# FFN layer 1 with fixed PSUM banks and a first output summed in PSUM, four layernorms on another engine, and shifted due times of the attention

## The chip, the core and the metric

The kernel runs on one core of a Trainium2 chip. The metric is the time of one execution in device microseconds (us), median of three runs. The core has five engines with a queue each, worked off strictly in the written order: TensorE (PE, with its weight loads, PEld), VectorE (DVE), ScalarE (ACT), GpSimd (POOL) and SyncE (SP), which issues nearly all DMAs. An instruction waits on semaphores that other engines or DMAs raise; everything behind it on its own engine waits with it.

## What is computed

The input x has 2048 tokens of 576 features. A parallel block is added to it:

```python
xn = layernorm(x)
out = x + A(xn) + B(xn)
# A: qkv = xn @ wqkv, 32 heads of 18; each token attends to itself and to
#    7 earlier tokens at distances 2, 4 .. 14; softmax; o @ wo
# B: h = xn @ w1 + b1 (4608 hidden); act = h * tanh(softplus(h)); act @ w2
```

Everything is float32. A product of two float32 matrices is made of three matmuls of rounded parts (high x high, low x high, high x low).

## The kernel before, in words

The tokens are worked in two halves (`hf` 0 and 1) of 1024, each of two blocks `b` of 512 tokens, each block of four tiles `jj` of 128. All matrix products run on PE; a schedule `plan`, a list of slots written out by hand, says in which order. A slot holds its PE work (`fns`) and background work (`before(i, fn)`: weight casts, attention steps, DMAs). The last loop of `block_kernel` walks the slots and emits, per slot, `first` (the exponentials that an attention step left for the next slot), then `bg`, then `held` (the activations that the slot before left in `pend`), then `fns`. For one slot, part 0 of quad (0, 1), `fns` comes ahead of `held`. At the end each engine is bound to this program order.

The stages, in order: a head (`prologue`, `first_item`) that normalises the first four tiles one by one (`ln_stats`, `ln_root`, `ln_newton`, `ln_norm`; lines 151 to 184), transposes them on PE (`ln_transpose`, `transpose_split`) and multiplies them by the first QKV weights; the rest of QKV; 18 quads of FFN; the second half's QKV, in part as `z_part`; 18 quads again; and the output projection (`wo_part`).

**A quad** (`hf, q`) is one 2x2 block product of FFN layer 1, computed with seven products of sub-blocks in place of eight. `m1_part` (line 715) issues it in six parts over three PSUM banks of 512 columns: `cur[1]`, `cur[2]`, `cur[3]`. Part 0 sums A11*B11 (6 matmuls, `prod`) in bank 1, ACT copies it to SBUF (`take`, line 691, "c11"), and A12*B21 with a rest (8 matmuls, `prod` and `rest`) goes into bank 2; then `mish` has DVE add c11 to bank 2 (line 702), ACT apply Mish with the bias (line 703), ACT round it to a high part (line 708) and POOL form the low part (line 709). Part 1 starts bank 3 (6 matmuls). Parts 2 and 3 go on in bank 1, with a copy each ("c21", "c22"); parts 4 and 5 finish banks 3 and 1. DVE's sums with c22 and c21 both read bank 3. Between the parts stand slots of FFN layer 2 of the quad before (`m2_pair`, line 755, or `p_item`, line 847, or `m2_cols`, line 868), whose sums DVE adds up (lines 759, 853, 871).

All these PSUM banks come from one tag "h" with four buffers, given out in turn as they come free; QKV, transposes, `z_part` and the projection use the same four. A second tag "out" has the other four.

**Attention** is a generator of 72 steps a half (POOL multiplies, lines 534 and 572; DVE reduces, lines 539 and 578; ACT exponential, line 559). The planner gives every slot a weight (`PART`, `US`), scales it by a `rate` for each stretch between `marks`, sums the weights up to `total`, and puts step n of 146 at the first allowed slot (`ok`) where the sum passes n/146 of the total, one step to a slot.

Of the kernel before, what the change touches and what calls it, by code (L numbers as in the profile page):

```python
# [39 lines left out]
def block_kernel(ctx: ExitStack, tc: tile.TileContext, x, wq, wo, w1, b1, w2, mask, out):  # L40
# [24 lines left out]
    warm = ps.tile([P, 512], F32, tag="h", bufs=4, name="warm")  # L65
# [3 lines left out]
    def transpose_split(src, dst, col, extra=None, pair=False):  # L69
        n = next(tpn)  # L70
        if pair:
            ta, tb = (ps.tile([P, 512], F32, tag="out", bufs=4, name=f"tt{k}_{n}") for k in range(2))
        else:
            ta = ps.tile([P, 512], F32, tag="h", bufs=4, name=f"ta_{n}")
            tb = ps.tile([P, 512], F32, tag="h", bufs=4, name=f"tb_{n}")
        for k in range(KT):
            nc.tensor.transpose(ta[:, k * P:(k + 1) * P], src[:, k * P:(k + 1) * P], ident)
# [5 lines left out]
        nc.scalar.copy(hi, tav)  # L83
        nc.vector.tensor_sub(dst[:, 5:5 + KT, col:col + P], tav, hi.bitcast(F32))
# [4 lines left out]
        nc.vector.tensor_sub(hr[64:P], tbv[64:P], hr[64:P].bitcast(F32))  # L89
# [74 lines left out]
    def ln_newton(n0):  # L164
        g = group[n0]
        k, rs, ve, y, nm = g["k"], *(g[w][:, 0:g["k"]] for w in ("rs", "ve", "y", "nm"))
        if k == 1:
            r, v, y, m = rs[:, 0], ve[:, 0], y[:, 0], nm[:, 0]
            nc.vector.tensor_scalar(y, r, r, v, op0=ALU.mult, op1=ALU.mult)
            nc.vector.tensor_scalar(y, y, -0.5, 1.5, op0=ALU.mult, op1=ALU.add)  # L170
            nc.vector.tensor_scalar(r, r, y, None, op0=ALU.mult)
            nc.vector.tensor_scalar(m, g["mv"][:, 0, 0:1], r, -1.0, op0=ALU.mult, op1=ALU.mult)
        else:
            newton(rs, ve, y)
            nc.vector.tensor_mul(nm, g["mv"][:, 0:k, 0:1], rs)
            nc.vector.tensor_scalar(nm, nm, -1.0, None, op0=ALU.mult)

    def ln_norm(n):
# [3 lines left out]
        nc.scalar.activation(xn[:, 0:D], accs[0][n], AF.Identity, bias=g["nm"][:, i, :], scale=g["rs"][:, i, :])  # L182
# [145 lines left out]
    def qkv_item(hf, g, b, jj, mid=None, mid_at=4):  # L328
# [7 lines left out]
        if (g, b, jj) == (NQ - 1, 0, JB - 1):  # L336
            pq = ps.tile([P, 512], F32, tag="out", bufs=4, name=f"pq_{n}_{jj}")
        else:
            pq = ps.tile([P, 512], F32, tag="h", bufs=4, name=f"pq_{n}_{jj}")
# [85 lines left out]
    def z_part(hf, jj, part):  # L425
        X0, X1 = XTs[hf, 0], XTs[hf, 1]
        tok = slice(jj * P, (jj + 1) * P)
        if part == 0:
# [5 lines left out]
            if jj == JB - 1:  # L434
                zq["h"] = [ps.tile([P, 512], F32, tag="out", bufs=4, name=f"z{n}_{jj}")[:, 0:432] for n in (1, 3)]
                zq["h"].append(ps.tile([P, 512], F32, tag="h", bufs=4, name=f"z2_{jj}")[:, 0:432])
            else:
                zq["h"] = [ps.tile([P, 512], F32, tag="h", bufs=4, name=f"z{n}_{jj}")[:, 0:432] for n in (1, 3, 2)]
# [211 lines left out]
    def bank(hf, q, n):  # L650
        cur[n] = ps.tile([P, TB], F32, tag="h", bufs=4, name=f"h{n}_{hf}_{q}")
        return cur[n]

    def prod(ph, wt, off, X, hi, lo, first, last):
        seq = [(off + k, wl, xs + k) for k in range(2) for wl, xs in ((0, hi), (0, lo), (1, hi))]
        for i, (wk, wl, xs) in enumerate(seq):
            nc.tensor.matmul(ph, wt[:, wl, wk * P:(wk + 1) * P], X[:, xs, :],  # L657
# [8 lines left out]
    seven = lambda hf, q: hf == 1 and q <= 2 * OC  # L666
    rawact, rslot, held_, owner, where = {}, {}, {}, {}, {}
# [47 lines left out]
    def m1_part(hf, q, part):  # L715
# [168 lines left out]
    def o_split(p, step, early=False):  # L884
        hf, j = divmod(2 * p, TJ)
        if step == 0:
# [4 lines left out]
            if early:  # L891
                od["t"] = [ps.tile([P, 512], F32, tag="h", bufs=4, name=f"ot{k}_{p}") for k in range(3)]
# [145 lines left out]
    def wo_part(p, part):  # L1038
# [8 lines left out]
        if part == 0:  # L1047
            od["h"] = [ps.tile([P, 512], F32, tag="h", bufs=4, name=f"o{n}_{p}")[:, 0:HC] for n in (1, 3, 2)]
# [127 lines left out]
    def prologue():  # L1176
# [19 lines left out]
    def first_item(n):  # L1196
# [3 lines left out]
        def mid():  # L1200
# [276 lines left out]
    for q in range(2 * OC + 2):  # L1477
        for i in range(spot(1, q, 0), spot(1, q, 9) + 1):
# [3 lines left out]
             spot(1, 2, 0), spot(1, 2 * OC + 2, 0), spot(1, NP - 1, 0), at["o", 0, 0], at["o", 2, 0]]  # L1482
    rate = (1.15, 0.4, 0.5, 0.8, 1.15, 1.3, 1.2, 0.8, 1.5, 0.8, 0)
# [4 lines left out]
    total = T[at["o", 2, 0]]  # L1488
# [95 lines left out]
```

## Time and profile before

| | us |
|---|---|
| median of 3 runs (lowest, highest) | 1124.1 (1123.77, 1124.33) |
| span of the profiled execution, first to last instruction | 1121.6 |
| median less span | 2.5 |
| PE busy / PEld busy | 1109.5 / 1023.0 |
| DVE busy / POOL busy / ACT busy | 829.0 / 787.7 / 492.1 |

How to read the lines that follow. The page groups instructions: line of the kernel, engine, operation, out<-in by the program's names, shape, count, then busy time and mean of one in ns, then the idle time of the engine just before. A row of the timeline has the start in us from the span's beginning, the duration, engine, line, operation and count; a bracket at its end tells how long the engine idled before and what ended that. A row of the waits says which engine and line waited for which other, us in total, how often, and the longest. Matmuls are pipelined: the duration of one includes its way through the array, while the next begins earlier.

### The profile page before, as it was taken

How to read it: one execution, taken by the hardware profiler on the slowest of the kernel's cores; microseconds unless marked ns; L12 is line 12 of the kernel's file. 1: busy time of each engine (PE TensorE's matmuls, PEld its weight loads, DVE VectorE, ACT ScalarE, POOL GpSimd, SP SyncE). 2: the span in 40 equal slices, each digit the busy share in tenths (PEclk: the TensorE clock that was granted, in tenths of full speed). 3: DMA queues.
4: the chain of work that ended last, by engine and by line, in shares of the span. 5: the costliest groups of instructions: out<-in, count | busy, mean ns of one | idle time of the engine just before them, and what ended most of it. 6: DMA issues, size and time to landing. Idle time of an engine off the chain costs nothing.

```text
span 1121.6 us, 18415 instructions
## 1 busy us (share of the span) xinstructions
PE 1109.5 (99%) x6630; PEld 1023.0 (91%) x6630; DVE 829.0 (74%) x1351; ACT 492.1 (44%) x892; POOL 787.7 (70%) x639
## 2 busy tenths in 40 slices
PE   8999999999999999999999999999999999999998
PEld 7999899999999999899999889999999999999998
DVE  6368788888888888877655456687866677776876
ACT  5544645544554545455233355343433343443332
POOL 2488767767689687676788476665789878668632
PEclk9999999999999999999999999999999999999999
DMA  6899885868767849666596797655655477676463
GB/s 200 283 312 318 290 283 205 289 228 284 261 240 258 282 163 345 222 240 214 191 342 238 231 373 249 241 200 174 227 198 189 168 263 269 215 253 248 157 222 104
DMA packets 147487, 271.08 MB, mean 242 GB/s; under 512 B 30114, under 2 KB 86724, under 8 KB 147396
## 3 DMA queue, kind: packets, MB, share of 16 engines
q1 hardware_dynamic: 147396, 269.91, 69.2%
q8 instruction: 52, 0.85, 0.3%
q14 instruction: 39, 0.32, 0.1%
HBM read 160.39 MB, written 109.48 MB: 241 GB/s over the span
## 4 chain that ended last, share of the span: by engine, by line
PE 89%; DVE 4%; POOL 3%; DMA 2%; issue 1%; ACT 1%; DVEq 0%; POOLq 0%; SPq 0%
PE h L657 28%; PE po L755 19%; PE pq L349 11%; PE po L868 10%; PE po L847 7%; PE h L663 5%; PE o L1056 4%; PE z L447 2%; DMA acc<-in_x 1%; POOL accP L856 1%; DVE u L801 1%; POOL pr L534 0%; DVE accP L871 0%; POOL act L709 0%; DMA z_B<-kept_wq 0%
## 5 line engine op out<-in xcount | busy, mean ns | idle before, releaser
L755 PEld LDWEIGHTS po<-w,act 128*128 128x128 f32 x1728 | 236.4, 188 | 7.5 <-DVE acc L759 1.7
L755 PE MATMUL po<-w,act 128*128 128x288 f32 x1728 | 240.8, 295 | 1.4 <-DVE acc L759 1.2
L534 POOL TENSOR_TENSOR pr<-q,kv 128x576 f32<-128x576 f32 x128 | 195.7, 1553 | 18.7 <-DMA q<-q_d 16.9
L572 POOL TENSOR_TENSOR pv<-L,kv 128x576 f32<-128x576 f32 x128 | 174.3, 1461 | 38.7 <-DVE L L565 20.9
L709 POOL TENSOR_TENSOR act<-c,act 128x512 fp32r<-128x512 f32 x81 | 107.1, 1322 | 128.4 <-ACT act L708 125.5
L759 DVE TENSOR_TENSOR acc<-po,acc 128x288 f32<-128x288 f32 x288 | 120.4, 450 | 31.6 <-PE po L755 30.2
L349 PE MATMUL pq<-wq,xt 128*128 128x432 f32 x672 | 136.2, 361 | 1.8 <-ACT xt L83 1.8
L868 PEld LDWEIGHTS po<-w,act 128*128 128x128 f32 x960 | 131.1, 188 | 3.7 <-DVE accP L871 0.4
L868 PE MATMUL po<-w,act 128*128 128x288 f32 x960 | 133.8, 295 | 0.2
L349 PEld LDWEIGHTS pq<-wq,xt 128*128 128x128 f32 x672 | 125.0, 188 | 8.7 <-ACT xt L83 2.7
L703 ACT ACTIVATE c<-c,b1c 128x512 f32<-128x512 f32 x81 | 58.7, 724 | 132.9 <-DVE c L702 132.6
L657 PE MATMUL h<-xt,t 128*128 128x512 f32 x432 | 110.6, 391 | 0.9 <-DVE c L702 0.8
L657 PE MATMUL h<-S,t 128*128 128x512 f32 x432 | 110.4, 391 | 0.0
L691 ACT COPY c<-h 128x512 f32<-128x512 f32 x81 | 47.4, 586 | 136.5 <-PE h L663 78.3
L578 DVE TENSOR_REDUCE og<-pv 128x144 f32<-128x1152 f32 x64 | 85.9, 1343 | 25.4 <-POOL pv L572 25.4
L657 PE MATMUL h<-xt,wa 128*128 128x512 f32 x432 | 104.0, 390 | 0.0
L657 PEld LDWEIGHTS h<-xt,wa 128*128 128x128 f32 x432 | 80.9, 188 | 16.9
L871 DVE TENSOR_TENSOR accP<-po,accP 128x288 f32<-128x288 f32 x160 | 69.6, 454 | 36.1 <-PE po L868 34.5
L847 PEld LDWEIGHTS po<-pw,u 128*128 128x128 f32 x672 | 92.4, 188 | 2.9 <-DVE u L801 0.5
L847 PE MATMUL po<-pw,u 128*128 128x288 f32 x672 | 94.2, 296 | 0.3 <-DVE u L801 0.3
L539 DVE TENSOR_REDUCE L<-pr 128x64 f32<-128x1152 f32 x64 | 85.8, 1341 | 11.2 <-POOL pr L534 11.1
L657 PEld LDWEIGHTS h<-xt,t 128*128 128x128 f32 x432 | 79.0, 188 | 16.1 <-DVE c L702 1.1
(231 smaller groups left out, 1840.5 us busy)
## 6 DMA issues: line engine op xcount, KB each, us to landing
kv<-kv_d SPq DMA_DIRECT2D x64, 396.0 KB, 5.2
kept_t<-t SPq DMA_DIRECT2D x36, 512.0 KB, 5.3
t<-kept_t SPq DMA_DIRECT2D x36, 512.0 KB, 5.4
rw<-in_w SPq DMA_DIRECT2D x36, 320.0 KB, 4.6
kept_wa<-wa SPq DMA_DIRECT2D x18, 640.0 KB, 3.5
kept_w<-w SPq DMA_DIRECT2D x20, 576.0 KB, 4.8
wa<-kept_wa SPq DMA_DIRECT2D x18, 640.0 KB, 6.1
w<-kept_w SPq DMA_DIRECT2D x20, 576.0 KB, 4.5
```

What stands on the lines that cost most here:

```text
L349: nc.tensor.matmul(pq[:, 0:432], XT[:, xi, tok], wt[wi][:, hl, 0:432], start=i == 0, stop=i == len(seq) - 1)
L534: nc.gpsimd.tensor_tensor(out=pr[:, x:x + hh], in0=q[:, j0 + x:j0 + x + hh, None, :].to_broadcast([P, hh, W, CU]), in1=win(kt, 0, CU, j0 + ...
L539: nc.vector.tensor_reduce(L[:, k, j0:j0 + hj].rearrange("p j w h -> p (j w h)"), pr.rearrange("p j w (h d) -> p (j w h) d", h=2), axis=AX, ...
L572: nc.gpsimd.tensor_tensor(out=pr[:, x:x + hj].rearrange("p j d w -> p j w d"), in0=L[:, k, x:x + hj, :, h:h + 1].to_broadcast([P, hj, W, DH]),
L578: nc.vector.tensor_reduce(og[:, :, c0:c0 + DH], pr, axis=AX, op=ALU.add)
L657: nc.tensor.matmul(ph, wt[:, wl, wk * P:(wk + 1) * P], X[:, xs, :], start=first and i == 0, stop=last and i == len(seq) - 1, skip_group_ch ...
L709: nc.gpsimd.tensor_tensor(out=a[:, 1, :], in0=t, in1=a[:, 0, :].bitcast(F32), op=ALU.subtract)
L755: nc.tensor.matmul(po, acts[hf, q, b, j][:, al, tok], done["w2", hf, 2 * q + j][:, wl, c * HC:(c + 1) * HC], start=i == 0, stop=i == 5)
L759: nc.vector.tensor_tensor(out=t, in0=po, in1=t, op=ALU.add)
L847: nc.tensor.matmul(po, units[e, k, qq][:, al, tok], w[:, qq, wl, :], start=i == 0, stop=i == 5)
L868: nc.tensor.matmul(po, acts[hf, q, b, j][:, al, tok], done["w2", hf, 2 * q + j][:, wl, c * HC:(c + 1) * HC], start=i == 0, stop=i == 5)
L871: nc.vector.tensor_tensor(out=t, in0=po, in1=t, op=ALU.add)
```

## The change

Three things are edited. First, the four "h" buffers become three tags: "h1" with two buffers, "h2" and "h3" with one each. Tiles with a role (n = 1, 2, 3) get their tag; all others take h1, h2, h1, h3 in turn. In quads with q >= 1 of half 0 and q >= 3 of half 1 ("seeded"), part 0 only sums A11*B11 and ACT copies it from bank 1 into bank 2; part 1 starts bank 3 and then adds A12*B21 and the rest onto the copy, and Mish reads the bank itself. In these quads `fns` of part 0 goes ahead of `held`, and the planner's weights of parts 0 and 1 change places. In quad (1, 0) the last two matmuls of A12*B21 and its rest move from part 0 to part 3, behind c22.

Second, tiles 0 to 3 are normalised by one DVE instruction in place of an ACT one, without the small instruction `nm`. In the prologue POOL's two first weight differences go behind tile 0's norm, and tile 0's norm ahead of tile 1's statistics; `ln_root(3)` and `ln_newton(3)` move from item 0 to item 1, behind tile 2's transposes.

Third, the planner's last mark and its rate of 0 are dropped, and the total ends at the projection's first slot.

```diff
+    HT = ("h1", "h2", "h1", "h3")
+    hturn = [0]
+    def h_tile(name, n=None):
+        if n is None:
+            tag = HT[hturn[0] % 4]
+            hturn[0] += 1
+        else:
+            tag = f"h{n}"
+        return ps.tile([P, 512], F32, tag=tag, bufs=2 if tag == "h1" else 1, name=name)
...
         if k == 1:
-            nc.vector.tensor_scalar(m, g["mv"][:, 0, 0:1], r, -1.0, op0=ALU.mult, op1=ALU.mult)
...
-        nc.scalar.activation(xn[:, 0:D], accs[0][n], AF.Identity, bias=g["nm"][:, i, :], scale=g["rs"][:, i, :])
+        if g["k"] == 1:
+            nc.vector.tensor_scalar(xn[:, 0:D], accs[0][n], g["mv"][:, i, 0:1], g["rs"][:, i, :], op0=ALU.subtract, op1=ALU.mult)
+        else:
+            nc.scalar.activation(xn[:, 0:D], accs[0][n], AF.Identity, bias=g["nm"][:, i, :], scale=g["rs"][:, i, :])
...
     def bank(hf, q, n):
-        cur[n] = ps.tile([P, TB], F32, tag="h", bufs=4, name=f"h{n}_{hf}_{q}")
+        cur[n] = h_tile(f"h{n}_{hf}_{q}", n)
...
+    seeded = lambda hf, q: q >= (1, 3)[hf]
...
         if part == 0:
             prod(bank(hf, q, 1), wa, 0, X0, 0, 5, True, True)
+            if seeded(hf, q):
+                nc.scalar.copy(bank(hf, q, 2), cur[1])
+                return
             take(hf, q, "c11")
-            prod(bank(hf, q, 2), wa, 2, X0, 2, 7, True, False)
+            prod(bank(hf, q, 2), wa, 2, X0, 2, 7, True, False, range(4) if (hf, q) == (1, 0) else range(6))
+            if (hf, q) == (1, 0):
+                return
             rest(cur[2], wa, 4, X0, 4)
             mish(hf, q, 0, 0, cur[2], cur["c11"])
         elif part == 1:
             prod(bank(hf, q, 3), t1, 0, X1, 0, 5, True, True)
+            if seeded(hf, q):
+                prod(cur[2], wa, 2, X0, 2, 7, False, False)
+                rest(cur[2], wa, 4, X0, 4)
+                mish(hf, q, 0, 0, cur[2])
...
             take(hf, q, "c22")
+            if (hf, q) == (1, 0):
+                prod(cur[2], wa, 2, X0, 2, 7, True, False, range(4, 6))
+                rest(cur[2], wa, 4, X0, 4)
+                mish(hf, q, 0, 0, cur[2], cur["c11"])
...
     def add(tag, *fns, alias=None):
-        plan.append((list(fns), [], PART[tag[3]] if tag[0] == "m" else US[tag[0]]))
+        part = tag[3] ^ 1 if tag[0] == "m" and tag[3] < 2 and seeded(tag[1], tag[2]) else tag[-1]
+        plan.append((list(fns), [], PART[part] if tag[0] == "m" else US[tag[0]]))
...
-        first_cast(0, nc.gpsimd)()
+        lows = [first_cast(0, nc.gpsimd)]
         ln_newton(0)
+        lows.append(first_cast(1, nc.gpsimd))
+        ln_norm(0)
+        for fn in lows:
+            fn()
         ln_stats(1)
-        low1 = first_cast(1, nc.gpsimd)
-        ln_norm(0)
-        low1()
...
             if n == 0:
                 ln_norm(2)
                 ln_stats(3)
+            if n == 1:
                 ln_root(3)
                 ln_newton(3)
-            if n == 1:
                 ln_norm(3)
...
-    rate = (1.15, 0.4, 0.5, 0.8, 1.15, 1.3, 1.2, 0.8, 1.5, 0.8, 0)
+    rate = (1.15, 0.4, 0.5, 0.8, 1.15, 1.3, 1.2, 0.8, 1.5, 0.8)
...
-    total = T[at["o", 2, 0]]
+    total = T[at["o", 0, 0]]
...
+    early = {at["m", hf, q, 0] for hf in range(NH) for q in range(NP) if seeded(hf, q)}
     for i, (fns, bg, _) in enumerate(plan):
...
-        for fn in first + bg + (fns + held if i == at["m", 0, 1, 0] else held + fns):
+        for fn in first + bg + (fns + held if i in early else held + fns):
```

(The list `marks` also loses its last entry, the projection's slot `("o", 2, 0)`. The calls for QKV, transposes, `z_part`, `o_split` and `wo_part` take their tiles from `h_tile`, with n where the code names h1, h2 and h3, in `z_part` and `wo_part`.)

More of the change, by code (lines that the diff above doesn't have):

```diff
@@ L73, in transpose_split @@
         else:
-            ta = ps.tile([P, 512], F32, tag="h", bufs=4, name=f"ta_{n}")
-            tb = ps.tile([P, 512], F32, tag="h", bufs=4, name=f"tb_{n}")
+            ta, tb = h_tile(f"ta_{n}"), h_tile(f"tb_{n}")
         for k in range(KT):
@@ L338, in qkv_item @@
         else:
-            pq = ps.tile([P, 512], F32, tag="h", bufs=4, name=f"pq_{n}_{jj}")
+            pq = h_tile(f"pq_{n}_{jj}")
         tok = slice(jj * P, (jj + 1) * P)
@@ L435, in z_part @@
                 zq["h"] = [ps.tile([P, 512], F32, tag="out", bufs=4, name=f"z{n}_{jj}")[:, 0:432] for n in (1, 3)]
-                zq["h"].append(ps.tile([P, 512], F32, tag="h", bufs=4, name=f"z2_{jj}")[:, 0:432])
+                zq["h"].append(h_tile(f"z2_{jj}", 2)[:, 0:432])
             else:
-                zq["h"] = [ps.tile([P, 512], F32, tag="h", bufs=4, name=f"z{n}_{jj}")[:, 0:432] for n in (1, 3, 2)]
+                zq["h"] = [h_tile(f"z{n}_{jj}", n)[:, 0:432] for n in (1, 3, 2)]
         h1, h3, h2 = zq["h"]
@@ L650, in bank, with prod @@
     def bank(hf, q, n):
-        cur[n] = ps.tile([P, TB], F32, tag="h", bufs=4, name=f"h{n}_{hf}_{q}")
+        cur[n] = h_tile(f"h{n}_{hf}_{q}", n)
         return cur[n]
-    def prod(ph, wt, off, X, hi, lo, first, last):
+    def prod(ph, wt, off, X, hi, lo, first, last, some=range(6)):
         seq = [(off + k, wl, xs + k) for k in range(2) for wl, xs in ((0, hi), (0, lo), (1, hi))]
         for i, (wk, wl, xs) in enumerate(seq):
+            if i not in some:
+                continue
             nc.tensor.matmul(ph, wt[:, wl, wk * P:(wk + 1) * P], X[:, xs, :],
@@ L891, in o_split @@
             if early:
-                od["t"] = [ps.tile([P, 512], F32, tag="h", bufs=4, name=f"ot{k}_{p}") for k in range(3)]
+                od["t"] = [h_tile(f"ot{k}_{p}") for k in range(3)]
             else:
@@ L1047, in wo_part @@
         if part == 0:
-            od["h"] = [ps.tile([P, 512], F32, tag="h", bufs=4, name=f"o{n}_{p}")[:, 0:HC] for n in (1, 3, 2)]
+            od["h"] = [h_tile(f"o{n}_{p}", n)[:, 0:HC] for n in (1, 3, 2)]
         h1, h3, h2 = od["h"]
```

6 lines of the change are left out of this document (3 added, 3 removed).

## The prediction, made before the result was known

> **What bounds the kernel now.** I read the page first, then the list of PE's waits, then the timeline where each wait stands.
>
> ```profile
> span 1121.6 us, 18415 instructions
> ```
> ```profile
> PE 1109.5 (99%) x6630; PEld 1023.0 (91%) x6630; DVE 829.0 (74%) x1351; ACT 492.1 (44%) x892; POOL 787.7 (70%) x639
> ```
>
> PE is busy for 1109.5 of 1121.6 us, and the change takes no matmul away and adds none. So time can come only from PE's waits, and any new wait of PE is paid in full. The list of waits (who waited <- for whom: us in total, times, longest) has, after two of the head:
>
> ```profile
> PE o L1056 <- DVE y L1060: 1.3, 2, 0.7
> PE po L755 <- DVE acc L759: 1.2, 1, 1.2
> PE ta L77 <- ACT xn L182: 0.9, 1, 0.9
> PE h L657 <- DVE c L702: 0.8, 1, 0.8
> PE h L657 <- ACT rt L691: 0.7, 1, 0.7
> PE po L847 <- DVE u L801: 0.3, 1, 0.3
> ```
>
> There is no wait that recurs from quad to quad: each is a single place. The steady pace of a quad shows in PE's timeline, and the length of one matmul in its group:
>
> ```profile
> 212.74 2.88 PE L657 MATMUL h<-xt,wa 128*128 128x512 f32 x12
> 215.46 0.62 PE L663 MATMUL h<-xt,wa 128*128 128x512 f32 x2
> ```
> ```profile
> L657 PE MATMUL h<-xt,wa 128*128 128x512 f32 x432 | 104.0, 390 | 0.0
> ```
>
> Twelve matmuls start in 2.72 us, 0.227 each, while one lasts 0.390. A shown wait counts from the modelled end, so PE loses 0.390 - 0.227 = 0.16 more than the row says; I add it, for the 288-column matmuls too.
>
> **The change, part by part.** *The sum on a copy.* DVE loses one addition of this kind in each of the 32 seeded quads, 22 us in all:
>
> ```profile
> L702 DVE TENSOR_TENSOR c<-h,c 128x512 f32<-128x512 f32 x81 | 55.4, 686 | 33.1 <-ACT c L691 17.9 <-PE h L663 14.2
> ```
>
> Beside PE's 99% that is worth nothing by itself; it counts only where PE waits for a late DVE. In exchange PE now needs the copy early: in part 0 the first bank ends after 6 matmuls, the third bank's 6 follow, then the first matmul on the copy. In the quad above that is due at 215.46, and ACT's copy, now into SBUF, stands so:
>
> ```profile
> 214.30 0.59 ACT L691 COPY c<-h 128x512 f32<-128x512 f32 x1
> ```
>
> It ends at 214.89, **0.57 us to spare**. No row shows ACT writing into PSUM. From below it costs nothing at all, from above ACT's dearest 512-wide row:
>
> ```profile
> L703 ACT ACTIVATE c<-c,b1c 128x512 f32<-128x512 f32 x81 | 58.7, 724 | 132.9 <-DVE c L702 132.6
> ```
>
> I take 0.59, the same operation; at 0.72 there are still 0.44 us left. So the copy is hidden, as long as ACT is free. The held Mish of the quad before no longer stands ahead of it, but the slot's `first` and `bg` do. The planner's arithmetic puts one half-0 exponential into a part-0 slot, quad (0, 4), where a weight cast follows it:
>
> ```profile
> 188.66 2.88 PE L657 MATMUL h<-xt,wa 128*128 128x512 f32 x12
> ```
> ```profile
> 190.86 0.42 ACT L559 ACTIVATE L<-L 128x256 f32<-128x256 f32 x1 [1.99 <-DVE L L555]
> 191.19 0.66 ACT L256 CAST w<-rw 128x576 fp32r<-128x576 f32 x1
> ```
>
> The copy starts at 191.85 and ends at 192.44; it is due at 188.66 + 2.72 = 191.38. Cost **+1.06** (0 if DVE releases the exponential 1 us sooner). What waits behind ACT here, Mish of the quad before and a table load, has slack: its result feeds a layer-2 slot several slots on.
>
> *Fixed banks.* With one buffer, bank 3 of a quad waits for DVE's second reading of bank 3 in the quad before. After most quads, a layer-2 slot, part 5 and part 0 lie between. Not so at (0, 1): quad (0, 0) has part 4 last, and no slot between.
>
> ```profile
> 114.75 2.88 PE L657 MATMUL h<-xt,wa 128*128 128x512 f32 x12
> ```
> ```profile
> 116.41 1.36 DVE L257 TENSOR_TENSOR t<-tt,t 128x512 fp32r<-128x512 f32 x1 [3.52 <-ACT t L256]
> 117.69 0.68 DVE L702 TENSOR_TENSOR c<-h,c 128x512 f32<-128x512 f32 x1
> ```
> ```profile
> 120.64 3.74 PE L755 MATMUL po<-w,act 128*128 128x288 f32 x24
> ```
> ```profile
> 126.08 3.35 PE L755 MATMUL po<-w,act 128*128 128x288 f32 x24
> 130.27 0.96 PE L657 MATMUL h<-xt,t 128*128 128x512 f32 x3 [0.85 <-DVE c L702]
> ```
>
> The sum at 117.69 is that reading, held up by a weight's low part. Bank 3 is free at 118.37; PE could begin it at 114.75 + 6 x 0.227 = 116.11. From 118.37, 6 + 8 + 6 matmuls lead to 122.91, where layer 2 now begins at 120.64: +2.27. Two waits go in return. The 24 matmuls took 3.74 instead of 3.35, since low parts came late: -0.39. At 130.27 PE waits for DVE: -(0.85 + 0.16) = -1.01, since POOL's weight differences, on which DVE's queue hangs there, now come ahead of the low part of the first activation (Mish is queued a slot later). Together **+0.87**; the ends are +0.2 (the low part runs uncontended, 0.68) and +2.3 (nothing comes back).
>
> *Waits that go.* The addition's place in DVE's queue, and one attention step that the swapped weights move from part 0 of quad (0, 15) to behind part 2, clear this backlog:
>
> ```profile
> 458.56 1.35 DVE L578 TENSOR_REDUCE og<-pv 128x144 f32<-128x1152 f32 x1 [2.40 <-POOL pv L572]
> ```
>
> DVE idled 2.40 us for POOL, then ran late up to PE's 1.2 us wait for L759. The reduction now comes a slot pair later: **-1.36** (0 if another reduction takes its place). At (1, 0) PE waits for c22:
>
> ```profile
> 636.10 1.19 PE L657 MATMUL h<-S,wc 128*128 128x512 f32 x4 [0.68 <-ACT rt L691]
> ```
>
> The four moved matmuls, 0.91 us, fill it: **-0.84** (part 2 now starts only 5 x 0.227 = 1.13 after bank 1's sixth matmul; by the rows at 212.74 and 214.30 a copy ends 1.02 after it: just enough; the ends are -0.84 and -0.3). At (1, 6) DVE's low part L801 stands behind the addition that vanishes:
>
> ```profile
> 747.21 0.69 DVE L702 TENSOR_TENSOR ra<-h,ra 128x512 f32<-128x512 f32 x1 [2.21 <-PE h L663]
> ```
>
> Without those 2.21 us of waiting the wait of 0.3 goes: **-0.46** (or 0).
>
> *The attention's end.* In both versions the weights from the projection's first slot on count nothing toward the total, so the due times stay; by the planner's arithmetic four of 146 steps move, by one to three slots, and the last two stay in the projection's first two slots. The two waits of L1056 for DVE, behind reductions such as this, stay:
>
> ```profile
> 1059.90 1.34 DVE L578 TENSOR_REDUCE og<-pv 128x144 f32<-128x1152 f32 x1
> ```
>
> Zero; the ends are 0 and -(1.3 + 0.32).
>
> *The head.* The first QKV matmul hangs on tile 1's statistics by way of ACT's Ln and Exp ahead of the cast of tile 0, so a faster norm of tile 0 gives nothing. No row shows a DVE norm; from below DVE's 1-element scalar form (0.15), from above its 576-wide form between SBUF tiles while POOL reads too (0.89):
>
> ```profile
> L313 DVE TENSOR_TENSOR twT<-twT,twhT 128x576 fp32r<-128x576 f32 x16 | 13.8, 894 | 0.3
> ```
> ```profile
> 10.76 0.82 DVE L114 BATCH_NORM_STATS2 st<-acc 128x6 f32<-128x288 f32 x2
> ```
> ```profile
> 14.56 0.82 DVE L114 BATCH_NORM_STATS2 st<-acc 128x6 f32<-128x288 f32 x2
> ```
> ```profile
> 14.75 0.60 PE L77 MATMUL ta<-ident,xn 128*128 128x128 f32 x4
> ```
> ```profile
> 16.64 0.60 ACT L83 CAST xt<-ta 128x512 fp32r<-128x512 f32 x1
> ```
> ```profile
> 15.66 0.15 DVE L160 TENSOR_SCALAR ve<-mv 128x1 f32<-128x1 f32 x1
> ...
> 16.81 0.21 DVE L171 TENSOR_SCALAR rs<-rs,y 128x1 f32<-128x1 f32 x1
> 17.06 0.22 DVE L172 TENSOR_SCALAR nm<-mv,rs 128x1 f32<-128x1 f32 x1
> 17.31 0.69 DVE L84 TENSOR_TENSOR xt<-ta,xt 128x512 fp32r<-128x512 f32 x1
> 18.03 0.29 DVE L89 TENSOR_TENSOR xt<-tb,xt 64x128 fp32r<-64x128 f32 x1
> ```
> ```profile
> 18.29 0.65 PE L77 MATMUL ta<-ident,xn 128*128 128x128 f32 x4
> ```
>
> I take 0.75, nearer the upper row: L702, which reads PSUM, takes 0.686 for 512 columns, and 0.75 allows for 64 more. Norm 1 then stands ahead of tile 2's statistics: without `nm` (0.25 with its gap) they start at 10.76 - 0.25 + 0.75 = 11.26, 0.50 late. Norm 2 runs from 14.56 - 0.25 + 0.50 = 14.81 to 15.56, so tile 2's transposes (0.60), due at 14.75 before, end at 16.2 and its cast (0.60) at 16.8. By this time tile 3's root used to be done; now it comes behind the low parts of tile 2: 0.69 + 0.29 and gaps, 17.87. From `ve` to the end of `rs` takes 17.02 - 15.66 = 1.36, which gives 19.23, and with the norm and a hand-over tile 3's transposes start at 20.02, against 18.29. PE has only four matmuls ahead of them and is full afterwards, so all of it is paid: **+1.73** (+0.1 with a norm of 0.15, +2.2 with 0.89). That tile 2's cast no longer stands behind tile 3's root only brings PE to this wait sooner.
>
> [...]
>
> **The sum:** 1.06 + 0.87 - 1.36 - 0.84 - 0.46 + 0 + 1.73 = +1.00 on the span of 1121.6. The median stands 2.5 above that span; I let that stand and add to the median: **1125.1**.
>
> **The rivals.**
> - *Copies late everywhere* (slower than before): if ACT reaches the copy over 0.57 us late, or a copy into PSUM takes over 1.16, PE pays the excess in every such quad. Against it: the row at 214.30 and the ceiling of 0.72. For it: ACT's queue holds casts that wait for POOL, and (0, 4) shows one. Half of the 32 quads late by 0.3: 1.00 + 4.8, **1129.9**.
> - *Only the old waits go*: no new one comes at (0, 1) and (0, 4), and the head breaks even: -1.36 - 0.84 - 0.46 - 0.39 - 1.01 = -4.06, **1120.0**. The queue order at 116.41 speaks against it.
> - *Norm 1 blocked by POOL*: in the new order POOL's weight differences fill the stretch to 12 us, such as
>
> ```profile
> 10.02 1.15 POOL L1173 TENSOR_TENSOR wq<-rq,wq 128x432 fp32r<-128x432 f32 x1
> ```
>
>   and if DVE's norm must wait one out, tile 1 and all behind it are 1.15 later: **1126.3**. DVE's low parts at L313 run slower than L702 does from PSUM, which speaks for it in part. [...]
> - *The attention does end earlier*, against my reading of the planner: 1.62 less, **1123.5**.
>
> **How the numbers follow.** Chances: forecast 0.55 (its own range 1122.8 to 1127.0, from the ends of its terms), copies late 0.20, only old waits go 0.10, norm blocked 0.10, attention earlier 0.05. The range 1121.8 to 1129.0 leaves out the fast rival and half of the slow one. About 0.2% (2.25 us) is what a measurement of this kernel can tell from no change. Faster: 0.10, the fast rival. Slower: 0.30, the slow rival with a tenth of the forecast and half of the blocked norm. Same: 0.60.
>
> **What would show it.** PE's waits after the change: one at L657 for DVE at quad (0, 1) of about 2.1 us; one at L657 for ACT's copy at (0, 4) of about 0.9; none for L759 in quad (0, 15), none for c22 at (1, 0); both of L1056 still there; tile 3's transposes at about 20.0. Wrong it would be if short waits of L657 for ACT's copy stand in many quads, if tile 3's transposes start before 18.3, or if bank 3 waits in quads other than (0, 1).

## The result, and the profile after

| | before | after |
|---|---|---|
| median us (lowest to highest; 22 runs each) | 1124.05 (1122.76 to 1126.27) | 1126.45 (1123.79 to 1128.99) |
| ratio of after to before, 95% interval | | 1.0018 (1.0011 to 1.0024) |
| span of the profiled execution | 1121.6 | 1124.8 |

The page of the changed kernel (span; busy time of the engines):

```profile
span 1124.8 us, 18311 instructions
...
PE 1110.1 (99%) x6630; PEld 1023.5 (91%) x6630; DVE 818.4 (73%) x1319; ACT 486.2 (43%) x888; POOL 790.7 (70%) x639
```

DVE lost 32 instructions and 10.6 us, PE's work is the same; the difference must stand in PE's waits. The list of PE's waits (total, times, longest):

```profile
PE h L671 <- DVE c L717: 2.2, 1, 2.2
PE ta L87 <- ACT wq L268: 1.8, 1, 1.8
...
PE o L1084 <- DVE y L1088: 1.3, 2, 0.7
PE h L671 <- DVE rt L717: 1.2, 1, 1.2
PE h L671 <- ACT h L740: 0.7, 1, 0.7
```

L671 is L657 of before, L740 the new copy into PSUM, L717 is L702, L87 is L77, and L1084 is L1056. Gone are the waits for L759 (1.2), for `c22` (0.7) and for the low part at (1, 6). The projection's two waits stay. New are the first, the second, the fourth and the fifth row. One row not shown, L875 (L847 of before) waiting 0.4 for L829 (L801 of before), isn't the wait at (1, 6) but the one that the ledger has at 824.

**Quad (0, 1).** The timeline of DVE and PE:

```profile
117.74 1.34 DVE L269 TENSOR_TENSOR t<-tt,t 128x512 fp32r<-128x512 f32 x1 [3.38 <-ACT t L268]
119.00 0.68 DVE L717 TENSOR_TENSOR c<-h,c 128x512 f32<-128x512 f32 x1
...
119.82 2.23 PE L671 MATMUL h<-xt,t 128*128 128x512 f32 x6 [2.22 <-DVE c L717]
121.85 2.55 PE L671 MATMUL h<-xt,wa 128*128 128x512 f32 x6
```

The sum that frees bank 3 ends at 119.68, behind a weight's low part, and PE starts bank 3 there. What follows is new: six matmuls last 2.55 us, where six starting at the usual 0.227 took 1.52. The windows view says why (columns: stretch; its length; busy us and instructions of PE, PEld, DVE, ACT and POOL; PEclk, the granted TensorE clock; the DMA share and GB/s):

```profile
117.19:120.60 3.41, 1.19 (x6) 0.68 (x5) 1.94 (x2) 3.06 (x6) 2.61 (x3) 1.00 0.93 301
120.61:124.02 3.41, 3.41 (x10) 2.65 (x9) 2.28 (x2) 1.68 (x3) 2.86 (x3) 0.50 0.86 348
124.03:127.44 3.41, 3.41 (x21) 3.03 (x20) 1.59 (x3) 2.42 (x5) 3.33 (x4) 1.00 0.45 183
```

From 120.61 to 124.02 the granted clock is 0.50. Nine matmuls start 0.427 apart there instead of 0.227: **1.8 us lost behind the wait**. Of the 22 runs, 11 have a mean granted clock of 0.998 or 0.997 over the span (median 1127.1) and 11 of 0.999 or more (median 1124.3). A stretch of 3.41 us at half clock lowers a mean over 1125 us by 0.0015. The two groups differ by 2.8, more than one stretch costs. Four of the low runs stand at 0.997, as the runs of E11 below do, whose profile has two stretches; what else sets the groups apart isn't recorded. Of 99 runs of the kernel before, made beside the experiments, none is below 0.999.

**The head**, DVE and PE:

```profile
17.38 0.15 DVE L170 TENSOR_SCALAR ve<-mv 128x1 f32<-128x1 f32 x1
...
18.54 0.21 DVE L181 TENSOR_SCALAR rs<-rs,y 128x1 f32<-128x1 f32 x1
18.79 0.58 DVE L192 TENSOR_SCALAR xn<-acc,mv,rs 128x576 f32<-128x576 f32 x1
...
19.52 0.63 PE L87 MATMUL ta<-ident,xn 128*128 128x128 f32 x4 [1.76 <-ACT wq L268]
```

Tile 3's root starts behind tile 2's low parts, and its transposes start at 19.52 (18.29 before). The bracket names ACT, but the norm at 18.79 is what ends just before (at 19.37). A norm on DVE takes 0.58.

**Quad (0, 4)**, ACT and PE:

```profile
194.64 0.42 ACT L571 ACTIVATE L<-L 128x256 f32<-128x256 f32 x1 [2.00 <-DVE L L567]
194.97 0.66 ACT L268 CAST w<-rw 128x576 fp32r<-128x576 f32 x1
195.53 0.58 ACT L740 COPY h<-h 128x512 f32<-128x512 f32 x1
...
196.16 1.65 PE L671 MATMUL h<-xt,wa 128*128 128x512 f32 x6 [0.71 <-ACT h L740]
```

The copy into PSUM stands behind the exponential and the cast, and lasts 0.58.

**Quad (1, 2)**, a place that the prediction doesn't name. DVE, POOL and PE after, then DVE and POOL before:

```profile
671.92 1.42 POOL L861 TENSOR_TENSOR accP<-accP,accP 128x576 f32<-128x576 f32 x1 [0.67 <-DMA accP<-in_x]
...
672.06 1.57 DVE L567 TENSOR_TENSOR L<-L,m 128x256 f32<-128x256 f32 x1
...
674.28 1.66 PE L671 MATMUL h<-xt,t 128*128 128x512 f32 x6 [1.17 <-DVE rt L717]
```
```profile
669.49 0.43 DVE L555 TENSOR_TENSOR L<-L,m 128x256 f32<-128x256 f32 x1
...
669.64 1.56 POOL L833 TENSOR_TENSOR accP<-accP,accP 128x576 f32<-128x576 f32 x1 [0.95 <-DMA accP<-in_x]
```

The same subtraction takes 0.43 us when it starts 0.15 ahead of POOL's addition, and 1.57 when it starts 0.14 behind it. At 674.28 PE waits because it goes on in bank 3, which DVE's late sum (L717) has yet to read. POOL starts when a DMA lands. In the 14 traces of this case POOL came first six times: the subtraction then took 1.20 to 1.63 and PE lost 0.97 to 1.36 here. The other eight times it took 0.42 to 0.43.

**The ledger**, us, each from PE's timeline as the distance of two neighbouring matmul starts less their usual distance:

| place | forecast | profiled |
|---|---|---|
| head | +1.73 | +1.23 |
| (0, 1): wait for bank 3 | +2.27 | +2.38 |
| (0, 1): half clock behind it | none | +1.8 |
| two old waits of (0, 1) | -0.39, -1.01 | -0.40, -1.12 |
| (0, 4): late copy | +1.06 | +0.98 |
| (0, 15); (1, 0); (1, 6) | -1.36; -0.84; -0.46 | -1.51; -0.95; -0.56 |
| attention's end | 0 | 0.0 |
| (1, 2): DVE behind POOL | none | +1.1 |
| two small ones at 824 and 829 | none | +0.25 |
| sum | +1.0 | +3.2 |

The spans differ by 3.2. The foreseen places alone sum to +0.05, the others to +3.15.

### The profile page after: what moved, and what is told of

It reads as the page before. It is cut to its first block, busy times and chain, and to the rows that moved or that the text cites. A ratio compares the mean times of both kernels' runs of the same rounds, so it can differ in the third digit from the quotient of the medians.

```text
span 1124.8 us, 18311 instructions
## 1 busy us (share of the span) xinstructions
PE 1110.1 (99%) x6630; PEld 1023.5 (91%) x6630; DVE 818.4 (73%) x1319; ACT 486.2 (43%) x888; POOL 790.7 (70%) x639
## 4 chain that ended last, share of the span: by engine, by line
PE 90%; DMA 3%; DVE 3%; POOL 1%; issue 1%; ACT 1%; SPq 0%; DVEq 0%; POOLq 0%
PE h L671 29%; PE po L783 20%; PE pq L361 11%; PE po L896 10%; PE po L875 7%; PE h L677 6%; PE o L1084 4%; PE z L459 2%; DMA kv_d<-zkv 1%; DMA pw<-kept_T 1%; POOL pr L546 0%; DMA wo<-wkept_T 0%; DMA y<-y_d 0%; PE ta L87 0%; DMA z_B<-kept_wq 0%
## 5 line engine op out<-in xcount | busy, mean ns | idle before, releaser
L724 POOL TENSOR_TENSOR act<-c,act 128x512 fp32r<-128x512 f32 x55 | 71.9, 1307 | 126.3 <-ACT act L723 123.2
L671 PE MATMUL h<-xt,t 128*128 128x512 f32 x432 | 111.2, 393 | 3.4 <-DVE c L717 2.2
L671 PE MATMUL h<-xt,wa 128*128 128x512 f32 x432 | 110.5, 393 | 0.7 <-ACT h L740 0.7
L671 PE MATMUL h<-S,t 128*128 128x512 f32 x432 | 110.4, 391 | 0.0
L671 PEld LDWEIGHTS h<-xt,wa 128*128 128x128 f32 x432 | 81.7, 190 | 18.3 <-ACT h L740 1.1
L671 PEld LDWEIGHTS h<-xt,t 128*128 128x128 f32 x432 | 79.3, 188 | 18.8 <-ACT h L740 2.6
L875 PEld LDWEIGHTS po<-pw,u 128*128 128x128 f32 x672 | 92.2, 188 | 2.9 <-DVE u L829 0.6
L875 PE MATMUL po<-pw,u 128*128 128x288 f32 x672 | 93.8, 295 | 0.4 <-DVE u L829 0.4
L706 ACT COPY c<-h 128x512 f32<-128x512 f32 x55 | 32.3, 587 | 137.9 <-PE h L677 80.5
L671 PEld LDWEIGHTS h<-S,t 128*128 128x128 f32 x432 | 77.8, 188 | 12.9 <-ACT ra L706 0.2
```

The source lines that it names most:

```text
L724: nc.gpsimd.tensor_tensor(out=a[:, 1, :], in0=t, in1=a[:, 0, :].bitcast(F32), op=ALU.subtract)
L875: nc.tensor.matmul(po, units[e, k, qq][:, al, tok], w[:, qq, wl, :], start=i == 0, stop=i == 5)
```

## The experiments

The theory: the change loses at (0, 1), in the head and at (0, 4), each by the order of a queue, and the two long waits lower PE's clock behind them. The rivals: the low clock has another cause; the copies into PSUM cost in general; the new places are only where a late engine shows. All kernels but E10 are edits of the changed kernel. "Low" counts the runs with a granted clock of 0.998 or below.

| | median us (lowest to highest; runs) | ratio to before (95% interval) | low |
|---|---|---|---|
| E1 (0, 1) as before | 1124.68 (1122.99 to 1125.73; 11) | 1.0005 (0.9996 to 1.0014) | 2 |
| E2 wait filled | 1124.91 (1123.66 to 1126.90; 11) | 1.0010 (1.0001 to 1.0019) | 3 |
| E3 copy (0, 4) first | 1126.59 (1124.22 to 1129.13; 11) | 1.0022 (1.0013 to 1.0031) | 8 |
| E4 root 3 first | 1125.24 (1123.66 to 1128.32; 11) | 1.0014 (1.0005 to 1.0023) | 6 |
| E5 t1 a slot earlier | 1125.14 (1122.49 to 1125.95; 11) | 1.0006 (0.9997 to 1.0015) | 5 |
| E6 root 3 first, other banks | 1124.11 (1122.60 to 1126.88; 11) | 1.0002 (0.9993 to 1.0011) | 4 |
| E7 no seeding | 1125.59 (1123.87 to 1127.72; 11) | 1.0015 (1.0006 to 1.0024) | 6 |
| E8 last steps behind | 1126.61 (1124.16 to 1127.46; 11) | 1.0020 (1.0011 to 1.0029) | 6 |
| E9 three repairs | 1122.12 (1121.20 to 1123.78; 11) | 0.9984 (0.9975 to 0.9992) | 0 |
| E10 before with new head | 1125.51 (1124.60 to 1127.13; 11) | 1.0016 (1.0007 to 1.0025) | 2 |
| E11 E9, steps doubled | 1129.07 (1127.61 to 1130.01; 5) | 1.0046 (1.0032 to 1.0060) | 5 |
| E12 E9, sum first | 1121.12 (1119.94 to 1123.47; 9) | 0.9980 (0.9970 to 0.9990) | 0 |

### E1: quad (0, 1) summed as before

```diff
-    seeded = lambda hf, q: q >= (1, 3)[hf]
+    seeded = lambda hf, q: q >= (2, 3)[hf]
...
-    early = {at["m", hf, q, 0]
+    early = {at["m", 0, 1, 0]} | {at["m", hf, q, 0]
```

> Quad (0, 1) is worked as in the kernel before (its first output is added from a copy in SBUF), everything else stays as changed. Theory: the loss at (0, 1) is the single third bank, which PE reaches after 6 matmuls instead of 14. With 8 matmuls (8 x 0.227 = 1.8 us) back in front, PE's wait there falls from 2.4 to about 0.6 us, the stretch at a granted clock of 0.5 behind it is gone, and the median falls by 1.8 + 1.8 = 3.6 to about 1122.8 us, with no run above 1125. Rival A (the low clock has nothing to do with the wait): the wait falls to 0.6 but a stretch at 0.5 is still there, median about 1124.6. Rival B (the bank isn't what PE waits for there): the wait stays over 2 us, median 1126.4.

PE's timeline:

```profile
132.60 1.65 PE L671 MATMUL h<-xt,t 128*128 128x512 f32 x6 [0.56 <-DVE c L717]
```

The wait for bank 3 fell from 2.38 to 0.59 and no low clock follows it in the profile, as forecast. The median is 1.9 above the forecast, three runs are above 1125 and two are low. The forecast took off the half clock in full, which only half of the runs have, and it left out that the seeding of (0, 1) had removed an old wait, which is back at 132.6 (0.72). In this profile (1, 2) cost 1.1, and norm 1 took 1.46, so that tile 3's transposes start at 20.52 (19.52 in the changed kernel). That the loss sits at (0, 1) stands; what undoing it gains was overrated.

### E2: the wait filled with idle matmuls

```diff
                 nc.scalar.copy(bank(hf, q, 2), cur[1])
+                if (hf, q) == (0, 1):
+                    spare = ps.tile([P, TB], F32, tag="out", bufs=4, name="spare")
+                    for k in range(8):
+                        nc.tensor.matmul(spare, wa[:, 0, 0:P], X0[:, 0, :], start=True, stop=True)
```

> The changed kernel with eight additional matmuls of 512 columns into an unused PSUM bank, between the first and the third bank's matmuls of quad (0, 1); their result is not used. PE is busy during the wait, and the wait for the bank stays as long as it was (8 x 0.227 = 1.8 of its 2.4 us are covered). Theory: the low clock follows from PE being idle, so the third bank's first matmul starts when it did (119.8 us), the stretch at 0.5 is gone, and the median falls by about 1.8 us to 1124.6, with no run above 1126. Rival (the low clock comes from something else): the stretch stays, median 1126.4 and the same spread from 1123.8 to 1129.

PE's timeline and a window:

```profile
119.80 1.63 PE L671 MATMUL h<-xt,t 128*128 128x512 f32 x6 [0.43 <-DVE c L717]
```
```profile
118.36:121.76 3.40, 2.97 (x14) 2.15 (x13) 1.33 (x3) 3.07 (x6) 2.04 (x3) 1.00 0.98 313
```

Bank 3 starts at 119.80 as in the changed kernel (119.82), yet the clock stays at 1.00, and the median fell by 1.5. That fits PE's idleness, not the wait or its end, as what brings the low clock. One profile alone can't show it, since E4's below stays at 1.00 with the wait unfilled; the windows in the last section, all but two, bear it out. Three runs are still low (11 of 22 in the changed kernel), against the forecast; where in them isn't recorded, but E10 shows a second place.

### E3: the copy of (0, 4) ahead of the exponential

```diff
+        if i == at["m", 0, 4, 0]:
+            order = fns + first + bg + held
```

> In quad (0, 4) alone, the work of part 0 with its copy into PSUM goes ahead of the exponential and the weight cast on ACT. Theory: PE's wait for the copy at 195 us (0.7 us by the list of waits, 0.98 by matmul starts) is gone, and nothing takes its place: median about 1125.4. Rival (the wait only moves, since the exponential and Mish that are now later feed PE as well): median 1126.4.

DVE and PE:

```profile
200.25 1.39 DVE L269 TENSOR_TENSOR wa<-rw,wa 128x640 fp32r<-128x640 f32 x1 [2.52 <-ACT wa L268]
...
202.54 1.54 DVE L787 TENSOR_TENSOR acc<-po,acc 128x288 f32<-128x288 f32 x4
...
203.04 1.18 PE L783 MATMUL po<-w,act 128*128 128x288 f32 x7 [1.28 <-DVE acc L787]
```

The wait for the copy is gone. ACT's casts come later instead, DVE stands behind one, and PE loses 1.44 at layer 2's sums, more than the 0.98 gained. The rival holds: with ACT the late engine here, another order on ACT only moved the wait.

### E4: root and norm of tile 3 back in item 0

```diff
                 ln_stats(3)
-            if n == 1:
                 ln_root(3)
```

> Tile 3's reciprocal root and its norm go back ahead of tile 2's low parts on DVE (root as in the kernel before, and the norm with it). Theory: the loss in the head is this order. Root 3 then ends at about 17.2 us, the norm at about 17.9, and tile 3's transposes start at about 18.0 instead of 19.5, with no later wait in the head: median about 1125.0 (1.4 less). Rival A (the low parts, now 0.6 us later, make PE wait instead): transposes at 18.0 and a new wait of 0.6 to 1.0 behind them, median about 1125.8. Rival B (ACT's cast of tile 2 behind the root holds PE up): a wait of about 0.7 ahead of the transposes and of 0.5 at them, median 1126.0.

ACT, then PE; and the two windows about (0, 1):

```profile
16.06 0.20 ACT L171 ACTIVATE rs<-ve 128x1 f32<-128x1 f32 x1 [2.96 <-DVE ve L170]
...
16.68 0.28 ACT L364 COPY qs<-pq 128x144 f32<-128x144 f32 x1
...
17.02 0.66 PE L87 MATMUL ta<-ident,xn 128*128 128x128 f32 x4 [1.89 <-DVE y L180]
...
19.57 0.60 PE L87 MATMUL ta<-ident,xn 128*128 128x128 f32 x4
```
```profile
115.02:118.43 3.41, 2.49 (x11) 1.72 (x10) 0.79 (x1) 3.31 (x7) 2.54 (x2) 1.00 1.08 362
118.43:121.84 3.41, 2.11 (x9) 1.80 (x10) 1.33 (x3) 3.09 (x6) 2.04 (x2) 1.00 0.95 331
```

No reason held. Tile 2's transposes now wait 2.05 us. The bracket names DVE, but what ends just before (at 16.96) are ACT's copies of tile 0's result (L364 the last, behind the root's Ln and Exp), which empty the PSUM bank that the transposes are given; in E9, with other banks, they start at 15.02. Tile 3's start at 19.57, no earlier. The lower median isn't the head's. The windows show how chance enters: the wait at (0, 1) is the same 2.38, but is split over two windows, PE busy for 2.49 and 2.11 us in them, and no low clock follows.

### E5: the low part taken from in front of the sum

```diff
-            ps_ = dict(raw=i, sums=i + 2, wa=i + 3, wc=i + 5, t0=i + 6, t1=i + 9)
+            ps_ = dict(raw=i, sums=i + 2, wa=i + 3, wc=i + 5, t0=i + 6, t1=i + 8)
```

> The changed kernel with one weight's cast (t1 of quad 1) a slot earlier, so that its low part no longer stands on DVE ahead of the sum that frees the third bank at (0, 1). Theory: that queue order is the whole loss at (0, 1). The sum then ends at about 116.9 us instead of 119.7, PE reaches the bank at 117.45 and does not wait; the 2.4 us and the stretch at a granted clock of 0.5 behind it go, without bringing the old waits of 0.4 and 1.1 back. By the undisturbed runs of the changed kernel (1124.2) that is 1121.8, with what is left of low-clock stretches about 1122.3, less than the kernel before. Rival (the cast is taken from Mish on ACT, or the low part's weight was what PE needed): a wait of 1 us or more is left, median 1125.

DVE, ACT and PE:

```profile
116.33 0.69 DVE L717 TENSOR_TENSOR c<-h,c 128x512 f32<-128x512 f32 x1 [1.26 <-PE h L677]
...
118.90 0.58 ACT L740 COPY h<-h 128x512 f32<-128x512 f32 x1
...
119.53 1.65 PE L671 MATMUL h<-xt,wa 128*128 128x512 f32 x6 [0.52 <-ACT h L740]
```

The sum ends at 117.02 (119.68) and bank 3 is no longer waited for: the queue order was the loss. Behind it stood a second one, 0.68: ACT reaches the copy only after three Mish of quad (0, 0). The median is 2.8 above the forecast; (1, 2) cost 1.0 in the profile, and five runs are low. The head is the one long wait left, though the place in those runs isn't recorded.

### E6: as E4, with other banks for tiles 2 and 3

```diff
-        transpose_split(xn, XTs[hf, b], jj * P, rem if b else None, (hf, b) == (1, 0) and jj < 3)
+        transpose_split(xn, XTs[hf, b], jj * P, rem if b else None, (hf, b) == (1, 0) and jj < 3 or (hf, b) == (0, 0) and jj > 1)
```

> Tile 3's root and norm back ahead of tile 2's low parts, and the transposes of tiles 2 and 3 in PSUM banks of the other tag, so that tile 2's no longer wait for the copies of tile 0's first QKV result. Theory: in the run with the root alone moved back, the bank took what the order gave. Now tile 2's transposes start at about 15.1 us and tile 3's at about 18.0 instead of 19.5: the head is 1.4 us shorter, its longest wait under 1 us, and fewer runs have a stretch at a low clock; median about 1124.6. Rival A (ACT's casts or the later low parts hold the QKV matmuls up instead): tile 3's transposes end where they did, at 20.0, median 1126. Rival B (the head's waits have no part in the low clock): head 1.4 us shorter, but as many runs at a clock of 0.998 and below as the changed kernel, about half.

In this profile tile 3's transposes start at 19.59, and the reason is the prediction's third rival. DVE and POOL, in the head and late in half 1, then the latter in the changed kernel:

```profile
10.51 1.53 DVE L192 TENSOR_SCALAR xn<-acc,mv,rs 128x576 f32<-128x576 f32 x1
10.59 1.13 POOL L1202 TENSOR_TENSOR wq<-rq,wq 128x432 fp32r<-128x432 f32 x1
...
906.75 5.60 POOL L546 TENSOR_TENSOR pr<-q,kv 128x576 f32<-128x576 f32 x4
907.51 5.46 DVE L985 TENSOR_TENSOR raw_T<-raw_T,woh_T 128x576 fp32r<-128x576 f32 x1
```
```profile
907.88 6.13 POOL L546 TENSOR_TENSOR pr<-q,kv 128x576 f32<-128x576 f32 x4
...
908.63 1.31 DVE L985 TENSOR_TENSOR raw_T<-raw_T,woh_T 128x576 fp32r<-128x576 f32 x1
```

Norm 1 met POOL's weight difference and took 1.53 (0.58 to 0.73 in eleven of the thirteen traces that have it, 1.46 and 1.53 in two). At 907 one DVE instruction stood beside four of POOL's for 5.46 us; in the other traces but E9's (5.50) it takes 1.30. PE lost 1.3 there. In E9 and E12, with the same head and norm 1 not held, tile 3's transposes start at 18.47 and 18.41. The median fell by 2.3, where 1.85 was forecast. Four of 11 runs are low, too few to tell from 11 of 22; that the head has a part in the low clock shows in E10.

### E7: no quad on a copy

```diff
-    seeded = lambda hf, q: q >= (1, 3)[hf]
+    seeded = lambda hf, q: False
```

> The changed kernel with no quad summed on a copy in PSUM: banks, norms and planner stay. Theory: seeding brings only what the ledger of waits shows. Gone: the wait at (0, 1) down by 1.8 and its low clock, the wait for the copy at (0, 4) by 1.0. Back: the waits at (0, 15) with 1.5 and at (1, 6) with 0.6, and some 0.7 behind (0, 1). Undisturbed runs 1124.2 - 2.8 + 2.8 = 1124.2, median about 1124.5. Rival A (the 22 us of DVE work saved count in many small places): slower than the changed kernel, over 1127. Rival B (the copy into PSUM costs in every quad): under 1122.5.

The list of waits has the old one again:

```profile
PE po L783 <- DVE acc L787: 1.2, 1, 1.2
```

By matmul starts 1.40 stand at (0, 15), 0.42 at (1, 6), and 0.59 and 0.71 at and behind (0, 1); the waits at (0, 4) and (1, 0) are absent. So seeding clears the first two, and the moved matmuls, which stay here, the one at (1, 0). The median lies between the forecast and the changed kernel; neither rival holds: 22 us of DVE work count only at those places, and the copies cost only at (0, 4) and (0, 1).

### E8: the last two attention steps behind the projection's work

```diff
-        before(k, lambda hf=hf: next(att[hf], None))
+        if k >= at["o", 0, 0]:
+            plan[k][0].append(lambda hf=hf: next(att[hf], None))
+        else:
+            before(k, lambda hf=hf: next(att[hf], None))
```

> The changed kernel with the last two attention steps behind the projection's work of their slots, instead of ahead of it. Theory: the two waits of the projection (0.76 and 0.85 us by matmul starts) are DVE's two last reductions standing ahead of its sums, so both waits go and the median falls by up to 1.6 to about 1124.9. Rival (the reductions only hold up the next sums and roundings, or the last output rows that wait for the attention): one or two waits of about the same size stand a slot later, median 1126.4.

PE's timeline:

```profile
1063.13 1.04 PE L1084 MATMUL o<-wo,oS 128*128 128x288 f32 x6 [1.05 <-DVE y L1088]
```

Two waits, this one of 1.21 and one of 0.62 by starts, where 0.76 and 0.85 stood: the rival. A reduction of 1.3 us finds no idle place on DVE there: from 1054 to 1068 its idle times are 0.44 us at most.

### E9: three repairs

E5 and E6 together, and DVE in ACT's place for the two copies that ACT reaches late:

```diff
+                copy = nc.vector.tensor_copy if (hf, q) in ((0, 1), (0, 4)) else nc.scalar.copy
+                copy(bank(hf, q, 2), cur[1])
```

> The changed kernel with the three repairs together: t1 of quad 1 cast a slot earlier; the copies into PSUM of quads (0, 1) and (0, 4) made by DVE, which idles there, instead of ACT, which is held up by Mish and by the exponential; tile 3's root and norm ahead of tile 2's low parts, with the transposes of tiles 2 and 3 in banks of the other tag. Theory: the changed kernel's three new losses (0, 1), (0, 4) and the head go, and with the two long PE waits every stretch at a low clock. From its undisturbed runs (1124.3): 2.4 + 0.95 + 1.2 less, 1119.8, with what DVE and POOL cost each other by chance about 1120.3, no run at a clock of 0.998 or below, and some 3.7 us (0.33%) faster than the kernel before. Rival A (the losses move on to later waits, as with the copy at (0, 4)): 1122 to 1123. Rival B (the low clock has other causes): a third or more of the runs still at 0.998 or below, median over 1121.5.

**Shorter than before** by 0.16% (interval 0.08 to 0.25), with no low run. (0, 4) has no wait left, since DVE's copy takes 0.70 while DVE is free. At (0, 1), DVE and PE:

```profile
116.44 0.70 DVE L741 COPY h<-h 128x512 f32<-128x512 f32 x1 [3.17 <-PE h L671]
117.05 0.68 DVE L717 TENSOR_TENSOR c<-h,c 128x512 f32<-128x512 f32 x1
...
117.87 1.63 PE L671 MATMUL h<-xt,t 128*128 128x512 f32 x6 [1.47 <-ACT act L723]
```

The copy waits 3.17 us for bank 1, and the sum that frees bank 3 stands behind it: PE loses 1.63. The bracket names ACT, but the sum ends at 117.73, just before PE starts. The forecast was 1120.3; the median is where rival A put it: the loss at (0, 1) moved into DVE's queue. In this profile PE also loses 1.37 behind the long L985 of E6.

### E10: the kernel before with the new head alone

The edit is the second part of the change, on the kernel before.

> The kernel before with the head of the change alone (norms of tiles 0 to 3 on DVE, POOL's differences behind norm 0, root 3 behind tile 2's low parts); banks, sums and planner as before. Theory: the head costs 1.2 us by itself, and its 1.9 us wait at tile 3's transposes is followed by a stretch at half clock in a part of the runs: a third or so at 0.998 or below, where the kernel before has none in 66. Median 1125.4. Rival A (only the wait at (0, 1) lowers the clock): no run below 0.999, median 1125.2. Rival B (in the rotating banks the new head costs nothing): 1124.1.

Windows of the head:

```profile
16.91:20.32 3.41, 1.63 (x11) 1.15 (x10) 2.74 (x9) 1.86 (x7) 0.77 (x2) 1.00 0.00 0
20.33:23.73 3.40, 3.40 (x11) 3.13 (x11) 1.16 (x3) 0.66 (x2) 0.33 (x1) 0.50 0.27 70
```

The median is 1125.51 where 1125.4 was forecast: the head alone makes the kernel before longer, and it has its own low clock: PE is busy for 1.63 of 3.41 us, and the next 3.4 run at 0.50. E7's profile has the same place (1.65 from 17.15, then 0.50). Two runs of eleven are low, where a third was expected.

### E11: E9 with the attention's end ahead of the projection

```diff
+        if n >= 2 * steps - 4:
+            k = at["o", 0, 0] - 2 + (n - 2 * steps + 4) // 2
```

> As the kernel with the three repairs, and the last four attention steps two to a slot in the two slots ahead of the projection, so that the attention does end ahead of it. Theory: the projection's two waits (0.76 and 0.85 us) are the two reductions of the last steps, so 1.6 us less than the repairs alone, about 1118.7. Rival (DVE has no idle time in the 12 us ahead of the projection, so its reductions there hold up layer 2's sums, or the projection's first sums all the same): no gain or a loss, 1120 to 1122.

The list of waits, and SP's row in the timeline:

```profile
PE ot L931 <- DMA o<-o_d: 3.4, 1, 3.4
```
```profile
1056.07 0.54 SPq L592 DMA_DIRECT2D o_d<-og  x1
1056.65 0.66 SPq L910 DMA_DIRECT2D o<-o_d  x1
```

A loss well past the rival's figure, by a queue that neither theory named. SP's store of the attention's last result now stands ahead of the projection's loads and waits for DVE's last reduction until 1056.07, so PE waits 3.4 us for a load; and DVE's two reductions make layer 2 wait 1.9. Both waits are followed by a half clock, hence 0.997 in all five runs.

### E12: E9 with the sum ahead of the copy

```diff
-    early = {at["m", hf, q, 0] for hf in range(NH) for q in range(NP) if seeded(hf, q)}
+    early = {at["m", hf, q, 0] for hf in range(NH) for q in range(NP) if seeded(hf, q) and (hf, q) != (0, 1)}
```

> As the kernel with the three repairs, but in quad (0, 1) the sums and activations held from quad (0, 0) go ahead of part 0's work, so that DVE's copy into PSUM stands behind the sum that frees the third bank. Theory: the 1.6 us that PE still lost at (0, 1) there is DVE's queue (its copy waits 3.2 us for bank 1, with the sum behind it). The sum then ends at about 115.9 us, the copy at 117.1, both before PE is due (116.2 and 117.6): no wait at (0, 1), 1.6 us less than with the three repairs, about 1120.5. Rival (PE waited there for something else, as ACT, which the list of waits names): the wait stays, 1122.1.

DVE's timeline:

```profile
115.03 0.69 DVE L717 TENSOR_TENSOR c<-h,c 128x512 f32<-128x512 f32 x1 [1.31 <-PE h L677]
116.39 0.70 DVE L741 COPY h<-h 128x512 f32<-128x512 f32 x1 [0.67 <-PE h L671]
```

The sum ends at 115.72, the copy at 117.09, and PE has no wait at (0, 1). The median fell by 1.0 from E9's, where 1.6 was forecast. At 1121.12 this is **0.20% below the kernel before** (interval 0.10 to 0.30), the best of all. One place gives 0.34 back (layer 1 at 129).

## Why the prediction was right, and where it wasn't

The median stands 0.18% above before (interval 0.11 to 0.24): at the edge of "within 0.2%", inside the range, 1.35 us over the forecast. Part of that nearness is luck: in the profile the foreseen places sum to +0.05 where +1.00 was forecast, and +3.15 that was not foreseen stands against it. The runs split 11 to 11 into low and others, so the median falls on the edge between the two groups.

- **Waits that go**: right, each within 0.15 us. E7 shows that seeding clears (0, 15) and (1, 6). Whether at (0, 15) it is the missing addition or the step that the swapped weights move stays open, since E7 undoes both.
- **Bank 3 at (0, 1)**: right in place, cause and size (2.27 forecast, 2.38 measured; E5). The step missed what can follow a long wait. It priced the wait by its own length, and PE's clock was taken as given: 1.8 us more in a part of the runs (E2, E4).
- **The copy at (0, 4)**: right (1.06, 0.98 measured). The ACT copy into PSUM takes 0.58, as one into SBUF (0.59). "Copies late everywhere" did not come (E7).
- **The head**: the mechanism was right, the size was 0.5 too high: a norm takes 0.58, not 0.75, and three of them stand in the sum. That the reorder is not simply a slip shows in E4: root 3 in item 0 makes tile 2's transposes wait for a bank.
- **The attention's end**: right, 0.0; E8 and E11 show that an earlier or later end costs as much or more.
- **Norm 1 blocked by POOL**, the third rival, is real, but a matter of chance: norm 1 took 1.46 and 1.53 in 2 of 13 traces, 0.58 to 0.73 in the others.
- **What was not in the sum**: the half clock, and the meeting of DVE and POOL at (1, 2), which in the trace of before went by chance in DVE's favour. The prediction named a wait for bank 3 in another quad than (0, 1) as a sign of being wrong, and (1, 2) is one. It isn't the fixed banks' doing: E10, with the old banks, loses 0.97 there. The runs of the changed kernel without a low clock have a median of 1124.3, 0.3 above before; how many of them paid at (1, 2) isn't recorded. **So the net of the foreseen places was near zero, and what makes the kernel longer is, for the most part, half clock behind two waits: with these waits shortened (E9, E12) no run of 20 is low.**

## What to carry to other kernels

At (0, 1) a PE wait of 2.38 us cost another 1.8 us in the profile, since a half clock followed it: look at the windows behind each long wait, and break a wait that can't be removed by work between, as E2 did. When a buffer gets fewer copies, look for what stands ahead of its last reader in that reader's queue, and when one instruction changes engine or place, ask the same of the new queue (E9, E11). A time that jumps between runs is worth explaining from their clocks before a median is read.

## What the runs showed of the hardware

**The clock.** In all 14 traces the granted clock changes only at distances that are whole multiples of 3.413 us: in the changed kernel at 4.55, 120.61 (34 of them later), 124.02 (1) and 1124.12 (293). In windows of that length, counted from these changes, it fell to 0.50 for one window behind those in which PE was busy for 0.12 us (E11, from 1059.42), 1.18 (E3, E6), 1.19 (above), 1.53 (E11), 1.63 (E10) and 1.65 (E7) of 3.41, and stayed at 1.00 behind 1.75 (E2, from 15.95), 1.88 (E3, from 17.93) and 2.11 (E4). An estimate from these numbers is a limit at about half a window. PE's busy time doesn't give it exactly: at the end of two profiles, where PE has no work left, 1.57 (E3) and 1.61 (E6) were not followed by it either. Where the windows lie differs from run to run (the one that holds the wait at (0, 1) begins at 117.19 in the changed kernel, at 116.69 in E6; in E4 one begins at 115.02 and the next at 118.43), so the same wait of 2.38 us was followed by a half clock that cost 1.8 us (the changed kernel) or by none (E4). The idle time within the window ahead of the half clock was 2.2 us at (0, 1) and, in the head, 1.8 us (E7, E10).

**DVE and POOL.** At (1, 2) L567's subtraction took 0.42 or 0.43 us where it came ahead of POOL's addition, and 1.20 to 1.63 behind it. Which comes first does not explain the two other cases. Norm 1 starts 0.20 to 0.38 ahead of POOL's difference in the eleven traces where it takes 0.58 to 0.73, and 0.03 and 0.08 ahead in the two where it takes 1.46 and 1.53. L985 starts 0.75 behind POOL's first multiplication in all 14 traces: in twelve it takes 1.30 us, in E6 and E9 5.46 and 5.50, until POOL's four are done (at 912.35 in E6, where L985 ends at 912.97). What decides there stays open.
